# Attention reciprocals spread by TensorE transposes, scores copied to SBUF with their maximum, q and k loaded in 256 B pieces

## The chip, the cores and the metric

One core of a Trainium2 chip runs the whole program. The metric is device time in microseconds of one execution. The kernel before takes 2468.42 us, the median of 3 runs (2465.64 to 2470.5).

## The reference

Three parts follow each other. The attention has 4 batches of 8 heads, 576 positions, 64 features, and keeps only the scores near the row's maximum:

```
scores = scale * q @ k^T
thresh = max(scores) - tau
scores = where(scores >= thresh, scores, -1e9)
attn   = exp(scores - max) / (sum + 1e-9);   out = attn @ v
```

Its output, as a matrix of 2304 x 512, goes through a gated feed-forward layer (512 to 1536 to 512, with SiLU), and then through a layer of 8 experts (512 to 1024 to 512) that are mixed with weights normalised 8 times over rows and columns. All in fp32. The kernel does products of fp32 precision with two or three matmuls on a high and a low part of each operand.

## The kernel before, in words

The attention runs over 16 pairs of heads. Four heads (two pairs) are a group for loading: `load` brings q, k and v of a group from memory in DMAs issued on SP's queue (L247 for the first 512 positions of q and k, L260 to L273 for the 64 left and for v). 512 positions lie as 128 partitions of 4 positions each, which gives runs of 1 KB in memory.

For each pair, `add_prep` makes the operands of the score product. `relaid` (L333) copies q and k in SBUF so that the two heads lie side by side, on GpSimd (for the first pair on VectorE). TensorE transposes (L348), ScalarE evicts, GpSimd splits into a high and a low part (L397, L403), and DMAs on SP's queue (`spread_q` L431, `spread_k` L436) put the parts of the two heads where the score matmuls need them (`qs`, `kk`).

A pair has 9 tiles of 128 query rows by 576 keys. For each tile `qk` (L463) writes the scores to two PSUM banks, `smax` (L468, VectorE) takes the negated maximum, `thresh` (L471, GpSimd) the threshold, `sexp` (L475, ScalarE) the exponentials, and `mask` (L484, VectorE) multiplies the exponentials by the comparison and sums the row. Maximum, exponential and mask all read the scores in PSUM; there are two pairs of banks, so the scores of tile t+2 wait for the mask of tile t. The masked tile is transposed on TensorE (L552), evicted on ScalarE (`ev`, by the helper L194), and is then the moving operand of the product with v (L635).

The sums lie along partitions, one per query, while the output has queries along the free axis. So the reciprocals are turned into a row: after tiles 3 and 8 of a pair GpSimd adds the small constant (L496), VectorE takes reciprocals (L542), TensorE transposes two columns at a time (`pe_rows`, L594, L596) into two PSUM rows, one for each head, ScalarE copies them to SBUF (`rr`, `row_act` L520), and `row_sp` (L511) issues two DMAs on SP's queue, each of which broadcasts one row to 64 partitions (`rb`, 96 or 64 KB). GpSimd multiplies the output by `rb` on its way to the feed-forward layer's operand `xT` (L649).

The order of the work is written by a planner. `sch.add(kind, engine, cost, fn, deps, ring, frees)` enters a task; `run` simulates five in-order engines with these costs and emits on each the first task that can start, with ties within 0.1 us broken by a key from the table `PLAN` (a base for each kind, a step for its number within a pair, and 17.5 for each pair). All engines run what they get in order, and so does SP's one DMA queue. Three rings of PSUM banks (two pairs of banks for scores, two banks for transposes, two for the rest) are part of the plan. A conversion of the first layer's weights from 64 bit, in 72 VectorE operations (L832 to L841) with DMAs of its own, is threaded through the attention.

Behind attention, `gate_val`, `down`, `up` and `mix` run the two layers with a TensorE stream of matmuls at L862 to L864. Nothing in them is changed.

Of the kernel before, what the change touches and what calls it, by code (L numbers as in the profile page):

```python
# [19 lines left out]
P = 128  # L20
# [6 lines left out]
    both=(-33.85, 5.8), cv=(5.32, 3.279), cvl=(18.47, 1.707), cvs=(-39.34, 0.904), den=(-79.39, 9.964),  # L27
    eload=(107.14, 8.319), ev=(35.38, 1.15), exp=(14.18, 1.348), load=(-17.63, 2.381), mask=(-13.56, 3.546),
    max=(-8.59, 2.113), open=(25.4, -10.09), pk=(3.96, 1.461), pkm=(-11.67, -0.917), pkt=(-1.23, 1.982),
    pq=(0.82, -0.319), pqm=(-14.65, -4.23), pqt=(-4.27, -2.076), prod=(125.51, 1.066), ptail=(-21.32, 2.621),  # L30
    pv0=(11.01, -1.752), pv1=(44.19, 0.926), qk=(-13.11, 1.766), rec=(4.5, 8.216), rel=(-13.23, 0.628),
    row=(16.67, 9.817), rowa=(36.19, 15.901), rows=(-45.07, 15.448), scale0=(62.75, -0.384),
    scale1=(69.78, -1.611), spread=(-64.72, 0.436), tail=(8.48, 12.06), tev=(46.97, 5.187), thr=(-10.82, 4.603),
    tr=(8.8, 0.242), u0=(-82.36, 2.843), u1=(50.51, 0.091), warm=(-60.47, 4.548), wh=(-33.08, -0.513),
    wl=(18.21, -5.451), xh=(85.01, 0.401), xl=(71.1, -1.867),
# [96 lines left out]
def attention_moe_moe_kernel(  # L132
# [60 lines left out]
    def copy_act(o, i):  # L193
        nc.scalar.activation(out=o, in_=i, func=AF.Copy)  # L194
# [10 lines left out]
    def attention():  # L205
# [33 lines left out]
        def load(g):  # L239
# [5 lines left out]
            def main(i, n):  # L245
                for nm, src in (("q", q), ("k", k)):
                    nc.sync.dma_start(  # L247
                        d[nm][:, 2 * i:2 * (i + n)].rearrange("p h r d -> p h (r d)"),
                        src[b, h0 + 2 * i:h0 + 2 * (i + n), 0:MAIN, :].rearrange("h (p r) d -> p h (r d)", r=NR),
                    )  # L250

            def qk_first():
                for nm in "qk":
                    d[nm] = raw_p.tile([P, 4, NR, D], F32, tag=f"r{nm}", name=f"r{nm}{g}")
                main(0, 1 if g == 0 else 2)
# [9 lines left out]
            def rest():  # L265
                d["v"] = rv_p.tile([P, 4, NR, D], F32, tag="rv", name=f"rv{g}")
# [10 lines left out]
                if g == 0:  # L277
                    main(1, 1)
# [40 lines left out]
        hls, spread, qk_last, raw_used, rel_used, whole = {}, {}, {}, {}, {}, {}  # L319

        def add_prep(p):
            g, i = divmod(p, 2)
            d = raw[g]
            src, tl = loads[g][1 if g == 0 and i else 0], loads[g][2]
            h = hls[p] = {}
            old, free = spread.get(p - 1, ()), qk_last.get(p - 2)

            def relaid(nm):

                def fn():  # L330
                    x = h["rel", nm] = raw_p.tile([P, NR, 2, D], F32, tag=f"rel{nm}", name=f"rel{nm}{p}", bufs=1)
                    eng = nc.gpsimd if p else nc.vector
                    eng.tensor_copy(x, d[nm][:, 2 * i:2 * i + 2].rearrange("p h r d -> p r h d"))  # L333
                return sch.add("rel", *(("POOL", 0.62) if p else ("DVE", 0.7)), fn, [src, rel_used.get(nm)])

            def banks(parts):
                def fn():
# [6 lines left out]
                    for nm, off in parts:  # L344
                        h["ps", nm] = t
                        if nm in "qk":
                            for r in range(NR):
                                nc.tensor.transpose(t[:, r * P:(r + 1) * P], h["rel", nm][:, r].rearrange("p h d -> p (h d)"), ident)  # L348
# [69 lines left out]
            rq, rk = relaid("q"), relaid("k")  # L418
            t0 = sch.add("ptail", "PE", 0.25, banks([("qt", 0), ("kt", P)]), [tl], ring=ring_v)
            t1 = rel_used["q"] = sch.add("pqm", "PE", 0.44, banks([("q", 0)]), [rq], ring=ring_v)  # L420
            t2 = rel_used["k"] = sch.add("pkm", "PE", 0.44, banks([("k", 0)]), [rk], ring=ring_v)
# [44 lines left out]
        def smax(t):  # L466
            stat[t] = u_p.tile([P, 2], F32, tag="stat", name=f"st{t}", bufs=6)
            nc.vector.tensor_reduce(stat[t][:, 0:1], sc[t], axis=AX.XY, op=ALU.max, negate=True)  # L468

        def thresh(t):  # L470
            nc.gpsimd.tensor_tensor(stat[t][:, 1:2], ntau, stat[t][:, 0:1], op=ALU.subtract)  # L471

        def sexp(t):
            ee[t] = e_p.tile([P, 2, HS], F32, tag="ee", name=f"ee{t}")
            nc.scalar.activation(out=ee[t], in_=sc[t], func=AF.Exp, bias=stat[t][:, 0:1], scale=1.0)  # L475

        def mask(t):
# [3 lines left out]
            if s % 2 == 0:  # L481
# [3 lines left out]
                m, sc.pop(t), stat.pop(t)[:, 1:2], ee.pop(t), op0=ALU.is_ge, op1=ALU.mult,  # L485
# [21 lines left out]
        def row_sp(p, c, box, w):  # L507
            def fn():
                rb = rbt[p, c] = u_p.tile([P, w], F32, tag=f"rb{c}", name=f"rb{c}_{p}", bufs=1 + c)
                for h in range(2):  # L510
                    nc.sync.dma_start(  # L511
                        rb[h * 64:(h + 1) * 64, :],
# [713 lines left out]
```

## Time and profile before

| | before |
|---|---|
| median of 3 runs | 2468.42 us |
| the profiled execution's own time | 2469.57 us |
| span of its instructions | 2466.1 us |
| granted TensorE clock, mean | 0.985 |
| TensorE busy | 2383.1 us |
| VectorE busy | 1068.2 us |
| ScalarE busy | 647.9 us |
| GpSimd busy | 566.0 us |

The busy time of an engine is the union of its instructions. The DMA share is the time in which the core's 16 DMA engines had packets under way, as a mean. All DMAs of this kernel are issued by SP and share one queue, which each DMA engine works off in order. The first 410 us or so are attention.

### The profile page before, as it was taken

The numbers are of one execution on the slowest core, as the hardware profiler recorded it, in microseconds if no ns is written. First come the engines' busy times: TensorE is split into PE (matmuls) and PEld (weight loads), VectorE is DVE, ScalarE is ACT, GpSimd is POOL, SyncE is SP. The second block draws the span as 40 slices with busy tenths as digits, with TensorE's granted clock in tenths as the row PEclk, the third lists the DMA queues.
The fourth block names the chain that finished last, engine by engine and source line by source line (L and its number), as shares of the span: only waits on it lengthen the run. The fifth ranks groups of instructions, "written<-read, shape, count | busy, mean of one in ns | idle before, by whom it ended". The sixth has DMA issues, their size and how long they took to land.

```text
span 2466.1 us, 31099 instructions
## 1 busy us (share of the span) xinstructions
PE 2383.1 (97%) x12925; PEld 2151.7 (87%) x12925; DVE 1068.2 (43%) x1731; ACT 647.9 (26%) x1154; POOL 566.0 (23%) x599
## 2 busy tenths in 40 slices
PE   7887888999999999999999999999999999999999
PEld 6665666999999989999999999999999999999998
DVE  5765775565854214433333333333333333333333
ACT  4765664332223321111111111111111111111110
POOL 3553543545546500110110010010011011001000
PEclk8998999999999999999999999999999999999999
DMA  8888984111111000000000000000000000000002
GB/s 201 164 140 133 143 130 78 39 39 39 44 35 52 21 10 13 26 18 27 26 18 26 13 24 20 14 29 15 26 26 18 26 26 18 26 13 31 1 1 77
DMA packets 74172, 112.64 MB, mean 46 GB/s; under 512 B 12720, under 2 KB 50608, under 8 KB 74032
## 3 DMA queue, kind: packets, MB, share of 16 engines
q1 hardware_dynamic: 74032, 110.67, 20.4%
q8 instruction: 101, 1.65, 0.3%
q14 instruction: 39, 0.32, 0.0%
HBM read 68.96 MB, written 7.08 MB: 31 GB/s over the span
## 4 chain that ended last, share of the span: by engine, by line
PE 90%; DMA 5%; SPq 1%; DVE 1%; POOL 1%; issue 1%; ACT 1%; POOLq 0%; DVEq 0%; ACTq 0%
PE h L862 11%; PE h L864 11%; PE h L863 11%; PE y L863 11%; PE y L864 11%; PE y L862 11%; DMA rb<-rr 3%; PE pv L635 2%; PE s L463 2%; PE d L864 2%; PE d L863 2%; PE d L862 2%; PE v L862 2%; PE v L864 2%; PE v L863 2%; PE g L862 2%
## 5 line engine op out<-in xcount | busy, mean ns | idle before, releaser
L1125 ACT ACTIVATE hh<-h 128x384 fp32r<-128x384 f32 x384 | 188.8, 492 | 1194.3 <-PE h L864 1194.3
L1126 DVE SCALAR_TENSOR_TENSOR hl<-h,hh 128x384 fp32r<-128x384 f32 x384 | 213.9, 558 | 629.4 <-ACT hh L1125 629.2
L1160 DVE SCALAR_TENSOR_TENSOR acc<-y,gate_p,acc 128x512 f32<-128x512 f32 x378 | 283.8, 751 | 357.7 <-PE y L864 357.6
L484 DVE SCALAR_TENSOR_TENSOR em<-s,st,ee 128x576 f32<-128x576 f32 x144 | 115.9, 814 | 61.1 <-ACT ee L475 37.0
L463 PE MATMUL s<-kk,qs 128*128 128x288 f32 x512 | 104.2, 331 | 36.9 <-DMA kk<-khl 16.0
L468 DVE TENSOR_REDUCE st<-s 128x1 f32<-128x576 f32 x144 | 108.0, 755 | 54.0 <-PE s L463 52.2
L999 POOL TENSOR_TENSOR al<-av,ah 128x384 fp32r<-128x384 f32 x72 | 88.7, 1232 | 181.4 <-ACT ah L194 181.4
L463 PEld LDWEIGHTS s<-kk,qs 128*128 128x128 f32 x512 | 77.6, 202 | 59.5 <-issue 38.6
L552 PE MATMUL t<-ident,em 128*128 128x128 f32 x576 | 93.5, 295 | 27.9 <-ACT rr L194 26.9
L475 ACT ACTIVATE ee<-s,st 128x576 f32<-128x576 f32 x144 | 105.8, 741 | 33.3 <-DVE st L468 26.3
L997 DVE TENSOR_TENSOR av<-v,s 128x384 f32<-128x384 f32 x72 | 40.0, 556 | 159.7 <-PE v L864 143.1
L552 PEld LDWEIGHTS t<-ident,em 128*128 128x128 f32 x576 | 74.2, 151 | 38.8 <-ACT rr L194 29.7
L194 ACT ACTIVATE et<-t 128x512 f32<-128x512 f32 x144 | 83.3, 596 | 39.4 <-PE t L552 38.4
L194 ACT ACTIVATE ah<-av 128x384 fp32r<-128x384 f32 x72 | 37.8, 525 | 158.6 <-DVE av L997 158.6
L635 PE MATMUL pv<-et,rv 128*64 128x320 f32 (+1 forms) x512 | 78.4, 436 | 0.0
L471 POOL TENSOR_TENSOR st<-ntau,st 128x1 f32<-128x1 f32 x144 | 36.3, 256 | 91.2 <-DVE st L468 73.4
L635 PEld LDWEIGHTS pv<-et,rv 128*64 128x64 f32 x512 | 33.4, 143 | 25.5 <-issue 11.7
L1022 DVE TENSOR_TENSOR x<-d,x 128x384 f32<-128x384 f32 x72 | 39.4, 554 | 35.6 <-PE d L864 35.6
L995 ACT ACTIVATE s<-g 128x384 f32<-128x384 f32 x72 | 34.7, 482 | 75.3 <-PE g L864 75.2
L649 POOL TENSOR_TENSOR xT<-u,rb 64x64 f32<-64x64 f32 (+2 forms) x71 | 34.0, 497 | 23.6 <-DMA rb<-rr 22.4
L1156 DVE TENSOR_TENSOR acc<-y,acc 128x512 f32<-128x512 f32 x36 | 24.9, 692 | 32.2 <-PE y L864 32.2
L1028 POOL TENSOR_TENSOR x2l<-x,x2h 128x1536 fp32r<-128x1536 f32 x6 | 21.0, 3503 | 24.4 <-ACT x2h L194 24.4
(862 smaller groups left out, 6892.0 us busy)
## 6 DMA issues: line engine op xcount, KB each, us to landing
kk<-khl SPq DMA_DIRECT2D x64, 320.0 KB, 6.1
raw_a<-in_moe_w_dram SPq DMA_DIRECT2D x16, 768.0 KB, 4.5
raw_b<-in_moe_w_dram SPq DMA_DIRECT2D x16, 768.0 KB, 4.6
qs<-qhl SPq DMA_DIRECT2D x64, 128.0 KB, 4.1
raw_g<-in_moe_w_gate_dram SPq DMA_DIRECT2D x6, 768.0 KB, 4.8
raw_v<-in_moe_w_val_dram SPq DMA_DIRECT2D x6, 768.0 KB, 4.7
raw_o<-in_moe_w_out_dram SPq DMA_DIRECT2D x6, 768.0 KB, 4.3
rv<-in_v_dram SPq DMA_DIRECT2D x8, 512.0 KB, 6.2
```

Source lines behind the costliest of these rows:

```text
L194: nc.scalar.activation(out=o, in_=i, func=AF.Copy)
L463: nc.tensor.matmul(ps[:, n, 0:HS], lhs, rhs[:, ko + n * HS:ko + (n + 1) * HS], start=(x == 0), stop=(x == len(ops) - 1))
L468: nc.vector.tensor_reduce(stat[t][:, 0:1], sc[t], axis=AX.XY, op=ALU.max, negate=True)
L484: nc.vector.scalar_tensor_tensor(m, sc.pop(t), stat.pop(t)[:, 1:2], ee.pop(t), op0=ALU.is_ge, op1=ALU.mult, accum_out=sums[p][:, s:s + 1],)
L552: nc.tensor.transpose(ps[:, kb * P:(kb + 1) * P], em[p, s // 2][:, o:o + P], ident)
L635: nc.tensor.matmul(o, lhs, rhs, start=(kb == 0), stop=(kb == NR))
L862: nc.tensor.matmul(ps, a[0], b[0], start=start, stop=False)
L863: nc.tensor.matmul(ps, a[0], b[1], start=False, stop=False)
L864: nc.tensor.matmul(ps, a[1], b[0], start=False, stop=stop)
L1125: nc.scalar.activation(out=hh[:, f], in_=t[:, 0:BLK], func=AF.Relu)
L1126: nc.vector.scalar_tensor_tensor(hl[:, f], t[:, 0:BLK], 0.0, hh[:, f].bitcast(F32), op0=ALU.max, op1=ALU.subtract)
L1160: nc.vector.scalar_tensor_tensor(a, t, gate_p[:, i * NTB + n, e:e + 1], a, op0=ALU.mult, op1=ALU.add)
```

## The change

Four things are changed, and with them all numbers of `PLAN`.

1. GpSimd writes each reciprocal 64 times into a tile `wide` (`widen`, a new task `bc`). TensorE transposes this, so that the row comes out on all 128 partitions at once, and ScalarE copies it to `rb`. `row_sp` and its DMAs are gone; the scaling waits for ScalarE's copy.
2. `smax` writes the negated scores to SBUF (`ns`, two buffers) in the operation that finds the minimum of them. The exponentials and the mask read that copy. The bank is given back after this operation; it waits for the mask two tiles before, and the score product waits for the score product one tile before.
3. q and k are loaded into tiles in which the two heads already lie side by side, by one DMA for each head, with runs of 256 B in SBUF. `relaid` is gone; the transposes read the loaded tile.
4. Each group's second pair is loaded in the third step of `load`, ahead of v, in the first group and in all others.

```diff
-    both=(-33.85, 5.8), cv=(5.32, 3.279), ...
+    bc=(13.34, 8.915), both=(-23.93, 4.248), cv=(4.31, 1.393), ...
...
-                    nc.sync.dma_start(
-                        d[nm][:, 2 * i:2 * (i + n)].rearrange("p h r d -> p h (r d)"),
-                        src[b, h0 + 2 * i:h0 + 2 * (i + n), 0:MAIN, :].rearrange("h (p r) d -> p h (r d)", r=NR),
-                    )
+                    for h in range(2):
+                        nc.sync.dma_start(
+                            d[nm][:, i, :, h, :],
+                            src[b, h0 + 2 * i + h, 0:MAIN, :].rearrange("(p r) d -> p r d", r=NR),
+                        )
...
-            a = sch.add("load", "SP", 2 * 0.65, one, old, land=4.5)
+            a = sch.add("load", "SP", 4 * 0.65, one, old, land=4.5)
-            c = sch.add("load", "SP", (3 if g else 5) * 0.65, three, [a, *v_use.get(g - 2, ())], land=6.0)
+            c = sch.add("load", "SP", 7 * 0.65, three, [a, *old, *v_use.get(g - 2, ())], land=6.0)
...
-                    eng = nc.gpsimd if p else nc.vector
-                    eng.tensor_copy(x, d[nm][:, 2 * i:2 * i + 2].rearrange("p h r d -> p r h d"))
...
-            nc.vector.tensor_reduce(stat[t][:, 0:1], sc[t], axis=AX.XY, op=ALU.max, negate=True)
+            x = e_p.tile([P, 2, HS], F32, tag="ns", name=f"ns{t}", bufs=2)
+            nc.vector.tensor_scalar(x, sc[t], -1.0, None, op0=ALU.mult, op1=ALU.min, accum_out=stat[t][:, 0:1])
+            sc[t] = x
-            nc.gpsimd.tensor_tensor(stat[t][:, 1:2], ntau, stat[t][:, 0:1], op=ALU.subtract)
+            nc.gpsimd.tensor_tensor(stat[t][:, 1:2], stat[t][:, 0:1], ntau, op=ALU.subtract)
-            nc.scalar.activation(out=ee[t], in_=sc[t], func=AF.Exp, bias=stat[t][:, 0:1], scale=1.0)
+            nc.scalar.activation(out=ee[t], in_=sc[t], func=AF.Exp, bias=stat[t][:, 0:1], scale=-1.0)
-                m, sc.pop(t), stat.pop(t)[:, 1:2], ee.pop(t), op0=ALU.is_ge, op1=ALU.mult,
+                m, sc.pop(t), stat.pop(t)[:, 1:2], ee.pop(t), op0=ALU.is_le, op1=ALU.mult,
...
-                    nc.sync.dma_start(
-                        rb[h * 64:(h + 1) * 64, :],
-                        box["row"][h:h + 1, :].rearrange("a (o n) -> a o n", o=1).to_broadcast([1, 64, w]),
-                    )
+            x = wide[p, c] = u_p.tile([P, 2, 2, 64], F32, tag="wide", name=f"wide{p}_{c}", bufs=2)
+            r = recip[p, c][:, 0:4].rearrange("p (r h o) -> p r h o", h=2, o=1)
+            nc.gpsimd.tensor_copy(x, r.to_broadcast([P, 2, 2, 64]))
...
-                box["row"] = u_p.tile([2, w], F32, tag=f"rrow{c}", name=f"rr{c}_{p}", bufs=1)
-                copy_act(box["row"], box["rt"])
+                rbt[p, c] = u_p.tile([P, w], F32, tag=f"rb{c}", name=f"rb{c}_{p}", bufs=1 + c)
+                copy_act(rbt[p, c], box["rt"])
...
-            k_ = sch.add("qk", "PE", 0.54 if s < 8 else 0.8, lambda: qk(t), [*sq, masks.get(t - 2)], ring=ring_s)
+            k_ = sch.add("qk", "PE", 0.54 if s < 8 else 0.8, lambda: qk(t), [*sq, qks.get(t - 1)], ring=ring_s)
-            m_ = sch.add("max", "DVE", 0.77, lambda: smax(t), [k_])
+            m_ = sch.add("max", "DVE", 0.84, lambda: smax(t), [k_, masks.get(t - 2)], frees=(k_,))
...
-                    nc.tensor.transpose(rt[:, o + r * P:o + (r + 1) * P], rc[:, 2 * r:2 * r + 2], ident)
+                    nc.tensor.transpose(rt[:, o + r * P:o + (r + 1) * P], wide[p, c][:, r].rearrange("p h n -> p (h n)"), ident)
...
-                "rowa", "ACT", 0.38 if c == 0 else 0.47, row_act(p, c, box, w), [R_, h_, rows.get((p - 1, c))],
+                "rowa", "ACT", 0.38 if c == 0 else 0.47, row_act(p, c, box, w), [R_, h_, rb_free.get((p - 1 - c, c))],
```

## Rows read from the trace of the kernel before

**Rows 1.** The page: busy time of the engines, and DMA in 40 slices.

```profile
PE 2383.1 (97%) x12925; PEld 2151.7 (87%) x12925; DVE 1068.2 (43%) x1731; ACT 647.9 (26%) x1154; POOL 566.0 (23%) x599
...
DMA  8888984111111000000000000000000000000002
```

**Rows 2.** Stretches: us, busy us (instructions) by engine, granted clock, DMA share, GB/s.

```profile
20.00:395.00 375.00, 307.65 (x2082) 229.64 (x2084) 258.77 (x528) 238.98 (x461) 183.72 (x417) 0.91 0.85 141
60.00:80.00 20.00, 18.36 (x136) 13.74 (x136) 18.52 (x36) 15.37 (x29) 12.13 (x28) 1.00 0.76 142
160.00:180.00 20.00, 19.99 (x150) 15.09 (x149) 17.29 (x35) 16.24 (x34) 13.21 (x33) 1.00 0.85 154
300.00:340.00 40.00, 38.89 (x288) 28.95 (x289) 34.68 (x71) 31.71 (x63) 24.44 (x58) 1.00 0.90 143
```

**Rows 3.** The chain of waits from 20 to 410 us, shares by line.

```profile
by line: DMA rb<-rr 17.0%; PE pv L635 14.8%; PE s L463 14.6%; PE t L552 9.3%; DMA kk<-khl 9.1%; SPq L511 3.9%; issue 3.9%; DVE st L468 3.2%; DVE em L484 2.5%; DMA rv<-in_v_dram 2.0%; SPq L436 1.9%; DMA stage<-first_v 1.9%; PE tp L348 1.8%;
```

**Rows 4.** Waits, 0 to 420 us: who waited for whom, us, times, longest us.

```profile
ACT rr L194 <- DMA rb<-rr: 33.9, 11, 8.8
PEld t L552 <- ACT rr L194: 29.7, 7, 8.2
...
PE s L463 <- DVE em L484: 17.2, 19, 3.8
```

**Rows 5.** Timeline at 105 us: start, us, instruction, idle before it.

```profile
105.12 1.11 PE L552 MATMUL t<-ident,em 128*128 128x128 f32 x4 [4.34 <-ACT rr L194]
```

**Rows 6.** DMA: 0:420 (two issues), 0:410, 380:384, 10:12, 14:16 (last two lines).

```profile
rb<-rr SPq DMA_DIRECT2D x32, 96.0 KB, 8.3
rb<-rr SPq DMA_DIRECT2D x32, 64.0 KB, 7.9
...
q1 hardware_dynamic: 40762, 57.49, 82.8%
...
q1 hardware_dynamic: 88, 0.11, 88.6%
...
q1 hardware_dynamic: 743, 0.73, 107.3%
...
DMA packets 926, 0.58 MB, mean 288 GB/s; under 512 B 588, under 2 KB 835, under 8 KB 926
...
q1 hardware_dynamic: 926, 0.58, 115.4%
```

**Rows 7.** Groups of instructions, 0 to 420 us: busy us, mean ns, idle before.

```profile
L484 DVE SCALAR_TENSOR_TENSOR em<-s,st,ee 128x576 f32<-128x576 f32 x144 | 115.9, 814 | 61.1 <-ACT ee L475 37.0 <-POOL st L471 21.7 <-POOL khl L397 0.4
L468 DVE TENSOR_REDUCE st<-s 128x1 f32<-128x576 f32 x144 | 108.0, 755 | 54.0 <-PE s L463 52.2
...
L484 DVE DVE_READ_ACCUMULATOR em<-s,st,ee 128x1 f32 x144 | 11.9, 82 | 0.0
...
L333 POOL COPY relk<-rk 128x512 f32<-128x512 f32 x15 | 9.7, 644 | 1.2 <-PE tp L348 1.1
...
L582 PEld LDWEIGHTS tt<-ident,em 128*128 128x128 f32 x64 | 8.7, 151 | 1.0 <-ACT et L194 0.5 <-issue 0.4
...
L491 POOL COPY em<-em 128x64 f32<-128x64 f32 x16 | 3.8, 237 | 1.0
```

**Rows 8.** VectorE with two SBUF inputs (min/median/max ns), and the timeline at 302 us.

```profile
L840 DVE TENSOR_TENSOR cr<-cr x9: 687/936/1332, 19.2 to 367.1; 128x512 f32<-128x512 f32 x9
...
L841 DVE SCALAR_TENSOR_TENSOR ct<-cr,ct x9: 674/683/980, 26.2 to 369.6; 128x512 f32<-128x512 f32 x9
...
302.11 1.27 POOL L403 TENSOR_TENSOR khl<-raw_k,khl 128x512 fp32r<-128x512 f32 x1
302.60 1.33 DVE L840 TENSOR_TENSOR cr<-cr 128x512 f32<-128x512 f32 x1
```

More of the change, by code (lines that the diff above doesn't have):

```diff
@@ L26 @@
 PLAN = dict(
[L27 to L35, printed above, removed]
+    bc=(13.34, 8.915), both=(-23.93, 4.248), cv=(4.31, 1.393), cvl=(-33.33, 3.759), cvs=(77.26, -4.782),
+    den=(3.32, 8.309), eload=(88.68, 8.021), ev=(50.95, 0.72), exp=(10.43, 4.099), load=(-33.65, 0.373),
+    mask=(-8.56, 2.817), max=(-17.16, 2.219), open=(77.15, -15.53), pk=(-10.38, 0.874), pkm=(-6.48, -1.78),
+    pkt=(2.08, 0.668), pq=(9.51, 2.909), pqm=(-9.12, -0.109), pqt=(3.38, -9.918), prod=(82.35, 5.49),
+    ptail=(-15.04, 10.369), pv0=(15.24, -2.732), pv1=(43.41, 1.62), qk=(-9.54, 2.196), rec=(9.02, 7.443),
+    row=(23.67, 11.733), rowa=(-106.02, 17.482), scale0=(49.08, 6.001), scale1=(58.83, 0.3),
+    spread=(-3.96, 0.861), tail=(10.05, 8.173), tev=(52.42, 6.252), thr=(-6.58, 4.734), tr=(9.48, 0.17),
+    u0=(35.84, -4.942), u1=(40.2, 1.375), warm=(-43.13, 3.335), wh=(36.26, -1.299), wl=(83.87, -5.771),
+    xh=(62.3, -2.254), xl=(52.73, 1.861),
 )
@@ L312, in add_load @@
             old = qk_use.get(g - 2, ())
-            a = sch.add("load", "SP", 2 * 0.65, one, old, land=4.5)
+            a = sch.add("load", "SP", 4 * 0.65, one, old, land=4.5)
             b_ = sch.add("load", "SP", 3 * 0.65, two, old, land=4.5)
-            c = sch.add("load", "SP", (3 if g else 5) * 0.65, three, [a, *v_use.get(g - 2, ())], land=6.0)
+            c = sch.add("load", "SP", 7 * 0.65, three, [a, *old, *v_use.get(g - 2, ())], land=6.0)
             loads[g] = (a, c, b_)
-        hls, spread, qk_last, raw_used, rel_used, whole = {}, {}, {}, {}, {}, {}
+        hls, spread, qk_last, raw_used, whole = {}, {}, {}, {}, {}
         def add_prep(p):
@@ L347, in fn @@
                             for r in range(NR):
-                                nc.tensor.transpose(t[:, r * P:(r + 1) * P], h["rel", nm][:, r].rearrange("p h d -> p (h d)"), ident)
+                                nc.tensor.transpose(t[:, r * P:(r + 1) * P], d[nm][:, i, r].rearrange("p h d -> p (h d)"), ident)
                         elif nm == "qt":
@@ L442, in add_prep @@
             whole[p] = qt, km, kt
-            qk_use[g] = [t0, rq, rk]
-        masks, exps, em_free, et_free = {}, {}, {}, {}
+            qk_use[g] = [t0, t1, t2]
+        masks, exps, qks, em_free, et_free = {}, {}, {}, {}, {}
         sc, stat, ee, em, sums, et = {}, {}, {}, {}, {}, {}
-        recip, rows, rbt = {}, {}, {}
+        recip, wide, rows, rbt = {}, {}, {}, {}
         def qk(t):
@@ L536, in add_tile @@
             b = 5 * p + s // 2
-            masks[t] = mk = sch.add("mask", "DVE", 0.9, lambda: mask(t), [th, x_, masks.get(t - 1), *em_free.get(b - 4, ())], frees=(k_,))
+            masks[t] = mk = sch.add("mask", "DVE", 0.9, lambda: mask(t), [th, x_, masks.get(t - 1), *em_free.get(b - 4, ())])
             em_free.setdefault(b, [])
```

45 lines of the change are left out of this document (18 added, 27 removed).

## The prediction

> **What bounds the kernel now.** I read the 40 slices first. DMA engines stand at 8 to 9 tenths in the first six slices and fall to 1 or 0 from the eighth nearly to the end, while TensorE is busy 97% of the whole span [rows 1]. So there are two parts: the attention stage, some 410 us, and the two feed-forward layers, in which TensorE has no gap. The change touches only the first. What the second part costs after that is taken as it is: it begins when attention's last products are out, so a microsecond saved in attention is one saved at the end.
>
> Then the stretches. From 20 to 395 us (375 us, from the first scores to the last mask) TensorE is busy 307.65 us at a mean granted clock of 0.91 (a mix of its levels of 1.2 and 2.4 GHz), VectorE 258.77, ScalarE 238.98, GpSimd 183.72; the DMA engines show 85% [rows 2]. Nothing computes all the time. Yet there are clean pieces, 60 to 80, 160 to 180 and 300 to 340 us, where the clock is 1.00 (2.4 GHz) and 574 matmuls (136, 150, 288) pass in 80 us, 7.18 per us. At that rate the 2082 matmuls of the whole stretch take 2082 / 7.18 = 290 us. So 85 us are lost in the pieces between.
>
> The chain of waits says to what. Of the chain from 20 to 410 us, 17.0% is the DMA `rb<-rr` (the broadcast of the reciprocal row) and 3.9% its issue on SP's queue, L511 [rows 3]: 20.9% of 390 us is 82 us, which meets the 85. The list of waits shows how it reaches TensorE: ScalarE's copy of the next row (`rr`, one buffer) waits 33.9 us for the broadcast that still reads the old one; ScalarE runs in order, so the score evictions behind that copy stop, and TensorE's transposes wait for PSUM banks, 29.7 us at the weight load [rows 4]. One case, at 105.12 us, is 4.34 us of idle TensorE [rows 5].
>
> The broadcasts are slow for what they carry. From 380 to 384 us only they run: 88 packets and 0.11 MB occupy 88.6% of 16 engines for 4 us, 0.11 / (4 x 0.886) = 31 GB/s. All 64 carry 32 x 96 + 32 x 64 KB = 5.24 MB [rows 6], 169 us of all 16 engines, out of 82.8% of 410 = 339 us in the stage [rows 6]. Half of the DMA time goes to an eleventh of the stage's 57.49 MB.
>
> **The change, part by part.**
>
> *Rows by transposes.* The 64 broadcasts go, and with them the wait of `rr`, the 82 us of the chain and 169 us of DMA time. GpSimd widens the reciprocals instead, 32 copies of 256 elements a partition; the nearest rows are copies of 64 elements, 237 ns, and of 512, 644 ns [rows 7], so 8 to 21 us, say 13, on an engine that is busy half of the stretch. TensorE makes as many transposes as before with 128 weight columns instead of 2, and ScalarE copies 128 partitions instead of 2 with the same elements per partition; both taken as zero (up to 80 x 0.15 = 12 us on TensorE were a whole weight load exposed each time, which the overlap of loads and matmuls speaks against). New waits: TensorE's row transposes wait for the widening (mask, GpSimd, VectorE, GpSimd, TensorE), with all later products behind them; ScalarE's row copy waits for the scaling of the previous pair that still reads `rb`, with evictions and exponentials behind it. The scaling is GpSimd's last step of a pair and no DMA stands in it any more.
>
> *Scores copied by the maximum.* TensorE's bank is free after the maximum, not after the mask: 17.2 us of `s` waiting for `em` [rows 4] go or shrink. They are inside the 85 us. The next maximum must wait for the mask two tiles earlier (two `ns` buffers), which VectorE has run anyway. The price is VectorE's. The maximum now also reads out its accumulator, which takes 82 ns where the mask does it [rows 7]: 144 x 0.082 = 12 us; if the body also grows from the reduction's 755 to the mask's 814 ns, 8 more. I take 12. The mask now has two tensor inputs in SBUF. Before, one came from PSUM. Its body could fall to 755 ns (8 us less). But rows of such operations spread: L840 takes 687 ns at least, 936 in the median and 1332 at most, L841 674, 683 and 980 [rows 8]; the 1.33 us one, at 302.60, began while GpSimd's 1.27 us subtraction from 302.11 ran [rows 8]. Excess of the median: 0.009 to 0.249 us; times 144, 1 to 36 us, and 93 us at L840's worst. I take the middle, 0.13 us, 19 us.
>
> The Trainium skill has a rule on this (SBUF — State Buffer, section "Who interferes with whom"): a VectorE instruction with two SBUF inputs contends with a GpSimd instruction that reads SBUF, and the later one waits until the first is through. The trace agrees in the pair at 302 us. By that rule GpSimd's small thresholds are also held up by masks, which the sum doesn't charge; what the rule would do at its worst is the slower rival below.
>
> *256 B loads.* The re-laying copies on GpSimd go, 30 of about 0.64 us [rows 7], 19 us for the 13 added; GpSimd is not late, so no gain. Each later group of two pairs loads q and k as 4096 packets of 256 B instead of 1024 of 1 KB. From 10 to 12 us, 1 KB packets: 107.3% x 2 x 16 / 743 = 46 ns each. From 14 to 16 us, 588 of 926 packets are small; 115.4% x 32 = 36.9 us less 338 x 46 ns leaves at most 36 ns for a small one [rows 6]; at the byte rate of the large ones it would be 11.5. Taken: 23 ns. A group goes from 1024 x 46 / 16 = 2.9 to 4096 x 23 / 16 = 5.9 us of all engines, 21 us over seven groups (nothing to 44). In one queue this stands in front of the spreads of q and k, which the matmuls wait for; with 169 us of broadcasts gone I charge a quarter as exposed, 5 us. SP issues 8 DMAs where it issued 2, but loses 8 broadcasts for the same group. The first group's extra loading and its two copies saved at the start are set against each other (3 us either way).
>
> The skill's page DMA: Bandwidth & Descriptors, "Specifications", says that transfers under 512 B don't reach the line rate; the packets from 14 to 16 us don't contradict it, and by it the upper end of 36 ns would be the likelier, and the sum 2427 instead of 2421.6 (a quarter of 44 us exposed, not of 21).
>
> **The sum.** TensorE could do the stretch in 290 us. VectorE now has 258.8 + 12 + 19 = 290 us of work, and is busy at best 18.52 of 20 us, 70.5 of 80 (88%) in the clean pieces [rows 2]. At 90% it needs 322 us: it is late next, not TensorE. So 375 becomes 322, a gain of 53, less 5 for the loads: 48. The profiled execution took 2469.57 us, so 2421.6; it is 1.2 above the median of the runs shown, 2468.42. Forecast 2421 us.
>
> **Rivals.** *TensorE stays the bound* (mask free of contention, loads hidden): the stretch falls to 290 us, 85 gained, 2385 us. For it: in the clean pieces TensorE is the fuller engine. Against: VectorE would have to be busy at 93% or more.
>
> *Loads clog the queue.* At 36 ns a packet a group costs 9.2 us, 6.3 more than before; seven of them wholly in front of spreads take 44 of the 53 us back: 2461 us. For it: spreads already wait in that one queue behind loads at 85% occupancy. Against: half of that occupancy leaves.
>
> *Slower: masks behind GpSimd.* Place: VectorE's mask, 144 times. At 0.55 us excess each (between L840's median and its worst) VectorE has 258.8 + 12 + 79 = 350 us of work; at 90% 389 us, 14 more than 375: 2483 us. It decides from (0.9 x 375 - 271) / 144 = 0.46 us per mask on. For it: GpSimd is busy 49% of the stretch. Against: L841, the nearest form, has a median only 9 ns over its least.
>
> *It doesn't do what it says*: TensorE waits for the widening as it waited for the broadcast. 32 row steps would have to lose 2.5 us each to eat 82 us; the new hop is one copy of under 0.65 us. Held in the second rival's chance.
>
> **Chances.** Forecast (2405 to 2440) 0.50, TensorE bound 0.20, loads 0.20, slower 0.10. What a measurement can tell from no change is 0.2%, 5 us. A little of the second and of the third rival's edge falls within: faster 0.87, same 0.04, slower 0.09. The range runs from 2388 to 2455: it takes in most of TensorE's case and the half-exposed loads, and leaves out the slower one.
>
> **What would show it.** Attention's last mask at about 345 us instead of 395; no chain share of `rb`; DMA share of the stage near 50 to 60%; the waits of `rr` and of `t` on ScalarE gone; VectorE at 85 to 93% and in the chain; the mask's mean at 0.8 to 1.05 us. The clock should be nearer to 1.00, since TensorE idles less. Wrong: if the mask's mean passes 1.27 us, if the spreads `kk` take more than 8 us to land in the middle of the stage, or if TensorE's row transposes carry long waits on the widening.

## The result, and the profile after

The changed kernel takes 2410.97 us (median of four runs, 2410.57 to 2413.97) where the kernel before took 2467.61 (2465.64 to 2470.5) beside it: a ratio of 0.9772, 95% interval [0.9755, 0.9789], 57 us less. The forecast was 2421 us, range 2388 to 2455. The profiled execution took 2410.57 us with a span of 2408.5 and a mean granted clock of 0.995 (before: 2469.57, 2466.1 and 0.985).

The page of the changed kernel, busy time and the DMA engines in 40 slices, against [rows 1]:

```profile
PE 2365.5 (98%) x12925; PEld 2141.9 (89%) x12925; DVE 1097.1 (46%) x1873; ACT 652.8 (27%) x1154; POOL 628.9 (26%) x601
...
DMA  8666632010110100000000000000000000000002
```

After the first slice the DMA engines stand at 6, not 8 to 9, and attention is over about a slice (60 us) earlier. TensorE has the same 12925 matmuls. VectorE has 29 us more work and GpSimd 63 us more, although GpSimd lost the 19 us of re-laying copies and gained only the 18 us of widening.

The last mask shows the end of attention. The row gives the mask's least, median and largest duration in ns, then first and last start in us:

```profile
L478 DVE SCALAR_TENSOR_TENSOR em<-ns,st,ee x144: 802/819/1870, 24.3 to 338.3; 128x576 f32<-128x576 f32 x144
```

The same of the kernel before:

```profile
L484 DVE SCALAR_TENSOR_TENSOR em<-s,st,ee x144: 798/817/820, 23.3 to 394.1; 128x576 f32<-128x576 f32 x144
```

The last mask starts at 338.3 us instead of 394.1. That is 55.8 of the 57.6 us by which the span is shorter, so the feed-forward layers behind it take as long as they did.

Stretches of the changed kernel (us; busy us and instructions of TensorE, its weight loads, VectorE, ScalarE, GpSimd; granted clock, DMA share, GB/s), against [rows 2]:

```profile
20.00:340.00 320.00, 291.96 (x2102) 220.96 (x2102) 284.83 (x668) 243.84 (x462) 249.46 (x424) 0.97 0.66 154
60.00:300.00 240.00, 224.14 (x1650) 170.41 (x1648) 217.89 (x508) 188.84 (x362) 194.46 (x334) 0.99 0.66 153
20.00:60.00 40.00, 31.96 (x198) 25.74 (x200) 29.92 (x75) 24.26 (x45) 25.14 (x43) 0.83 0.91 210
```

What took 375 us takes 320. VectorE is busy 284.83 / 320 = 89% and GpSimd 78% (before 69% and 49% of the 375). In the middle, 1650 / 240 = 6.88 matmuls pass per us. The first 40 us are still slow: 198 matmuls at a granted clock of 0.83, DMA engines at 91%. The middle piece of the kernel before, for the comparisons below, is 1385 / 240 = 5.77 per us:

```profile
60.00:300.00 240.00, 201.31 (x1385) 148.13 (x1384) 164.53 (x335) 156.64 (x304) 122.11 (x280) 0.92 0.87 145
```

The chain of waits from 20 to 352 us, shares by line, against [rows 3]:

```profile
by line: PE s L454 10.1%; PE pv L626 9.5%; issue 7.9%; POOL xT L640 6.6%; PE t L544 6.6%; DMA kk<-khl 5.2%; POOL st L465 4.7%; POOL khl L395 4.4%; POOL qhl L395 4.3%; POOL qhl L389 3.4%; ACT ee L469 3.0%; SPq L427 3.0%; DVE em L478 2.5%; PO
```

No broadcast is left in it. In its place stand small shares of everything, and GpSimd (xT, st, khl, qhl) has 23.4% in this one line, VectorE's mask 2.5%.

Waits of the changed kernel from 0 to 360 us (us, times, longest us), against [rows 4]:

```profile
POOL st L465 <- DVE ns L461: 52.0, 49, 21.6
...
ACT rb L194 <- PE tr L588: 16.5, 9, 8.0
PEld s L454 <- DVE ns L461: 14.1, 20, 1.3
...
PEld tr L586 <- POOL wide L505: 10.2, 10, 1.9
...
PE tr L586 <- POOL wide L505: 7.7, 7, 1.7
```

The waits of `rr` for the broadcast and of `t` for `rr` are gone. The new hop over GpSimd's widening shows 10.2 us of waits at the weight load and 7.7 at the matmul, never over 1.9 us at once.

Groups from 0 to 360 us (busy us, mean ns, idle before), against [rows 7]:

```profile
L478 DVE SCALAR_TENSOR_TENSOR em<-ns,st,ee 128x576 f32<-128x576 f32 x144 | 138.3, 960 | 12.6 <-POOL st L465 8.2 <-ACT ee L469 3.6 <-POOL qthl L389 0.3
L461 DVE TENSOR_SCALAR_CACHE_REDUCE ns<-s 128x576 f32<-128x576 f32 x144 | 108.3, 752 | 17.2 <-PE s L454 11.2
L465 POOL TENSOR_TENSOR st<-st,ntau 128x1 f32<-128x1 f32 x144 | 67.9, 471 | 53.4 <-DVE ns L461 52.0
L505 POOL COPY wide<-rec 128x256 f32<-128x256 f32 x32 | 18.2, 569 | 5.5 <-DVE rec L533 4.2 <-PE s L454 0.4 <-PE t L544 0.4
L389 POOL TENSOR_SCALAR qhl<-raw_q 128x512 fp32r<-128x512 f32 x15 | 14.2, 948 | 0.0
L461 DVE DVE_READ_ACCUMULATOR ns<-s 128x1 f32 x144 | 11.6, 81 | 0.0
```

The mask has grown from 814 to 960 ns, its least and median have not (802 and 819): a part of the 144 is held up, one for 1870 ns. The maximum that also copies 576 scores a partition has the body of the plain one, 752 against 755 ns, plus an accumulator read of 81 ns. GpSimd's threshold, one element a partition, went from 256 to 471 ns, and the high part of q (L397 before) from 647 to 948.

DMA of the changed kernel, 0 to 350 us (packets, MB, share of 16 engines), against [rows 6]:

```profile
q1 hardware_dynamic: 61088, 52.97, 64.7%
```

64.7% of 350 us is 226 us of 16 engines, where it was 339.

### The profile page after: what moved, and what is told of

It is laid out like the page before. It is cut to its first block, busy times and chain, and to the rows that moved or that the text cites. A ratio compares the mean times of both kernels' runs of the same rounds, so it can differ in the third digit from the quotient of the medians.

```text
span 2408.5 us, 31221 instructions
## 1 busy us (share of the span) xinstructions
PE 2365.5 (98%) x12925; PEld 2141.9 (89%) x12925; DVE 1097.1 (46%) x1873; ACT 652.8 (27%) x1154; POOL 628.9 (26%) x601
## 4 chain that ended last, share of the span: by engine, by line
PE 90%; POOL 5%; issue 1%; DMA 1%; ACT 1%; DVE 1%; SPq 1%; POOLq 0%; DVEq 0%; ACTq 0%
PE h L853 11%; PE h L855 11%; PE h L854 11%; PE y L854 11%; PE y L855 11%; PE y L853 11%; PE d L854 2%; PE d L855 2%; PE d L853 2%; PE v L853 2%; PE v L854 2%; PE v L855 2%; PE g L853 2%; PE g L854 2%; PE g L855 2%; PE s L454 1%
## 5 line engine op out<-in xcount | busy, mean ns | idle before, releaser
L478 DVE SCALAR_TENSOR_TENSOR em<-ns,st,ee 128x576 f32<-128x576 f32 x144 | 138.3, 960 | 12.6 <-POOL st L465 8.2
L469 ACT ACTIVATE ee<-ns,st 128x576 f32<-128x576 f32 x144 | 111.6, 775 | 32.1 <-DVE ns L461 31.2
L461 DVE TENSOR_SCALAR_CACHE_REDUCE ns<-s 128x576 f32<-128x576 f32 x144 | 108.3, 752 | 17.2 <-PE s L454 11.2
L544 PE MATMUL t<-ident,em 128*128 128x128 f32 x576 | 85.6, 280 | 3.1 <-ACT et L194 2.2
L465 POOL TENSOR_TENSOR st<-st,ntau 128x1 f32<-128x1 f32 x144 | 67.9, 471 | 53.4 <-DVE ns L461 52.0
L544 PEld LDWEIGHTS t<-ident,em 128*128 128x128 f32 x576 | 67.9, 143 | 11.6 <-ACT et L194 5.3
L640 POOL TENSOR_TENSOR xT<-u,rb 64x64 f32<-64x64 f32 (+2 forms) x71 | 46.0, 661 | 4.4 <-ACT u L194 3.2
```

The source lines that it names most:

```text
L461: nc.vector.tensor_scalar(x, sc[t], -1.0, None, op0=ALU.mult, op1=ALU.min, accum_out=stat[t][:, 0:1])
L478: nc.vector.scalar_tensor_tensor(m, sc.pop(t), stat.pop(t)[:, 1:2], ee.pop(t), op0=ALU.is_le, op1=ALU.mult, accum_out=sums[p][:, s:s + 1],)
L544: nc.tensor.transpose(ps[:, kb * P:(kb + 1) * P], em[p, s // 2][:, o:o + P], ident)
```

## The experiments

Theory: the broadcasts are the loss, and taking them away is the whole gain; copied scores and small packets cost what the sum charges. Rivals: the copied scores free banks and carry part of the gain; VectorE's contention sets the new end; or the time is made by the planner, which writes a new order for every edit. The last one had no term in the prediction, and the runs brought it up.

Twelve kernels ran, each with runs of the kernel before beside it on the same chip (before: 2466.6 to 2469.8 us).

| kernel | median us | ratio to before [95%] |
|---|---|---|
| the changed kernel | 2410.97 | 0.9772 [0.9755, 0.9789] |
| a1: changed, rows by DMA | 2498.88 | 1.0121 [1.0106, 1.0136] |
| a2: changed, scores in PSUM | 2435.81 | 0.9865 [0.9849, 0.9882] |
| a4: changed, mask reads PSUM | 2430.85 | 0.9847 [0.9832, 0.9861] |
| b1: before, rows by transposes, old table | 2473.38 | 1.0023 [1.0014, 1.0032] |
| d3: before, rows by transposes, new table | 2429.54 | 0.9849 [0.9835, 0.9862] |
| d1: changed, old table | 2457.46 | 0.9963 [0.9949, 0.9977] |
| p1: changed, 1 KB runs | 2407.28 | 0.9763 [0.9750, 0.9776] |
| c1: changed, threshold on ScalarE | 2468.31 | 1.0004 [0.9995, 1.0013] |
| r1: before, rows by transposes, same order | 2407.89 | 0.9756 [0.9742, 0.9771] |
| r3: changed, rows by DMA, same order | 2495.78 | 1.0113 [1.0098, 1.0128] |
| r2: changed, threshold on ScalarE, same order | 2405.02 | 0.9744 [0.9728, 0.9761] |
| r4: whole change, order of before | 2436.07 | 0.9864 [0.9844, 0.9884] |

### a1, a2, a4: parts of the change undone

a1 gives the changed kernel its broadcasts back:

```diff
-            nc.gpsimd.tensor_copy(x, r.to_broadcast([P, 2, 2, 64]))
+                    nc.sync.dma_start(
+                        rb[h * 64:(h + 1) * 64, :],
+                        box["row"][h:h + 1, :].rearrange("a (o n) -> a o n", o=1).to_broadcast([1, 64, w]),
+                    )
```

> The changed kernel with the reciprocal rows brought to the partitions by DMA broadcasts again; scores copied to SBUF and 256 B loads stay. Theory (the broadcasts are the loss: 64 of them hold the DMA engines about 169 us and ScalarE behind them): the stretch goes back to 375 us or more, 2465 to 2490 us, DMA share of the stage 0.85 or more, ScalarE's row copy waits for the broadcast again. Rival (the gain is the PSUM bank given back at the maximum): most of the gain stays, 2425 to 2440 us.

Measured 2498.88 us: 88 more than the changed kernel, 30 more than before, and 9 above the range that was expected. The planner wrote a new order for it, so these figures price the broadcasts and an order together; r3 below holds the order. One expected sign didn't come: ScalarE's row copy never waits for a broadcast here. GpSimd's scaling does, 27.1 us in all.

a2 leaves the scores in PSUM until the mask:

```diff
-            nc.vector.tensor_scalar(x, sc[t], -1.0, None, op0=ALU.mult, op1=ALU.min, accum_out=stat[t][:, 0:1])
-            sc[t] = x
+            nc.vector.tensor_reduce(stat[t][:, 0:1], sc[t], axis=AX.XY, op=ALU.max, negate=True)
```

> The changed kernel with maximum, exponentials and mask reading the scores in PSUM again, the bank held until the mask; rows by transposes and 256 B loads stay. Theory (once the broadcasts are gone VectorE and GpSimd are the bound, and the copy costs VectorE 12 us of accumulator reads and 21 us of mask, and GpSimd much more): mask back at 814 ns, threshold on GpSimd back near 256 ns, GpSimd busy under 190 us, time equal or better, 2385 to 2412 us. Rival (the bank given back early carries part of the gain): TensorE waits for the mask, 2425 to 2445 us.

a4 keeps the copy for the exponential, but the mask reads the scores in PSUM, so that it has one SBUF input; the bank is held until the mask:

```diff
-                m, sc.pop(t), stat.pop(t)[:, 1:2], ee.pop(t), op0=ALU.is_le, op1=ALU.mult,
+                m, scp.pop(t), stat.pop(t)[:, 1:2], ee.pop(t), op0=ALU.is_ge, op1=ALU.mult,
```

> The changed kernel in which only the mask reads the scores in PSUM again (exponentials still read the copy), so that the mask has one SBUF input and the bank is held until the mask. Theory (the mask's second SBUF input is what slows it and GpSimd): mask 960 to about 815 ns, GpSimd's threshold 471 to about 260 ns, GpSimd busy in the stretch 249 to under 200 us; the time follows whichever is larger, the 21 us of VectorE won or the bank held longer: 2390 to 2425 us. Rival (GpSimd is slower for another reason, its own added work): threshold stays above 400 ns.

2435.81 and 2430.85 us, 25 and 20 more than the changed kernel; the first is in the rival's range, the second above both ranges. In these two, VectorE's relief is worth less than what came with it. But both were planned anew, so the times alone don't say whether held banks or the order did it. What a4 does settle is the contention. Its groups from 0 to 360 us:

```profile
L478 DVE SCALAR_TENSOR_TENSOR em<-s,st,ee 128x576 f32<-128x576 f32 x144 | 116.1, 814 | 31.7 <-ACT ee L469 14.6 <-POOL st L465 13.5 <-POOL khl L389 2.1
...
L465 POOL TENSOR_TENSOR st<-ntau,st 128x1 f32<-128x1 f32 x144 | 31.4, 221 | 99.3 <-DVE ns L461 90.7 <-DVE rec L532 7.8
...
L389 POOL TENSOR_SCALAR qhl<-raw_q 128x512 fp32r<-128x512 f32 x15 | 9.7, 650 | 0.5
```

With one SBUF input the mask is back at 814 ns, and GpSimd's threshold falls from 471 to 221 ns, its high part of q from 948 to 650. a4 also holds the bank longer and has another order, so here are the thresholds one by one (least, median and largest ns), of the changed kernel and then of a4:

```profile
L465 POOL TENSOR_TENSOR st<-st,ntau x144: 179/627/752, 23.4 to 336.7; 128x1 f32<-128x1 f32 x144
```

```profile
L465 POOL TENSOR_TENSOR st<-ntau,st x144: 183/192/742, 24.2 to 354.1; 128x1 f32<-128x1 f32 x144
```

Sorted by when they start, the traces leave no room for the order as the cause. In the changed kernel 69 thresholds start while a mask runs and take 698 ns in the median; the 75 others take 189. The medians inside a mask are 698 to 701 ns in all six kernels with two SBUF inputs and the threshold on GpSimd (the changed one, a1, d1, p1, r3, r4), and 189 to 192 in all six whose mask has one (before, a2, a4, b1, d3, r1). Nor does any mask of the latter six take over 820 ns, while every kernel with two inputs has masks over 1800. So the mask's second SBUF input is what slows both engines, and the order sets how often they meet. The Trainium skill (SBUF — State Buffer, section "Who interferes with whom") says that a VectorE instruction with at most one SBUF input, outside its two-port modes, doesn't contend with GpSimd, and that one with two SBUF inputs contends with a GpSimd instruction that reads SBUF. These rows agree with it.

### b1, d3, d1: the rows alone, and the planner's table

b1 does the rows alone on the kernel before, with its table of keys and a guessed key for the new task; d3 is b1 with the table of the changed kernel; d1 is the changed kernel with the old table.

```diff
 PLAN = dict(
+    bc=(5.0, 8.5),
...
-    r_ = sch.add("rowa", "ACT", ...)
-    rows[p, c] = sch.add("rows", "SP", 1.3, row_sp(p, c, box, w), [r_, rb_free.get((p - 1 - c, c))])
+    bc = sch.add("bc", "POOL", 0.35, lambda: widen(p, c), [rec])
+    rows[p, c] = sch.add("rowa", "ACT", ..., row_act(p, c, box, w), [R_, h_, rb_free.get((p - 1 - c, c))])
```

> The kernel before with one part of the change alone: reciprocals widened on GpSimd and transposed by TensorE, no broadcasts. Theory: all or more than the whole gain, 2385 to 2415 us, since VectorE keeps its 259 us of work. Rival (only the parts together gain): 2435 to 2460 us.

> The kernel before with the rows by transposes alone, but with the new table of keys (the old key for the re-laying). Scores in PSUM until the mask, 1 KB loads with re-laying. Theory (rows plus an order that suits them is the larger half): 2425 to 2445 us, near the 2436 of rows and 256 B loads without the copied scores. Rival (rows without the other parts gain nothing in any order): 2460 to 2480 us.

> The changed kernel with the old table of keys (and a key of 5.0, 8.5 for the new widening): same work, another order. Theory (the order written by the planner is a bound of its own once the broadcasts are gone; rows alone with the old table gained nothing, TensorE taking the products with v of two pairs in one run of 40 while VectorE waited): most of the gain is lost, 2445 to 2475 us, with VectorE's masks waiting for TensorE. Rival (the order matters little, the parts carry the gain together): 2405 to 2425 us.

b1 was a miss for the theory and above the rival's range too: 2473.38 us, no gain at all, though no broadcast is left and the DMA share of 20 to 340 us fell to 0.54. d3, the same work in another order, takes 2429.54. d1, the whole change in an order by the old table, takes 2457.46, 46 more than the same work by the new one. Waits of b1, 0 to 380 us:

```profile
POOL rec L496 <- DVE em L484: 50.1, 16, 4.7
...
DVE em L484 <- PE tt L579: 41.5, 12, 4.3
```

and one such wait in its timeline (start, us):

```profile
99.92 1.14 PE L549 MATMUL t<-ident,em 128*128 128x128 f32 x8 [0.53 <-ACT et L194]
...
101.27 0.44 PE L579 MATMUL tt<-ident,em 128*128 128x128 f32 x2 [0.20 <-ACT et L194]
...
101.70 0.82 DVE L484 SCALAR_TENSOR_TENSOR em<-s,st,ee 128x576 f32<-128x576 f32 x1 [3.16 <-PE tt L579]
```

In this order TensorE's tail transposes (`tt`) come late, here behind 16 transposes of masked scores and 4 of the next pair's operands. They free the buffer that the next mask writes, so the masks wait 41.5 us for them. The same wait takes 33.8 us in d1 and 59.6 in c1 below, the other two orders that lose most or all of the gain; before, the changed kernel and d3 don't have it. That it makes the whole loss isn't shown. (The expectation of d1 blames a run of 40 products with v. b1 and d1 have such runs, but c1 has none over 20.) So a planned comparison prices two things at once, and an edit has to be priced with the order held.

### r1 and r3: the rows with the order held

For these, the order in which a kernel issues its operations was recorded and replayed. r1 is the kernel before with the rows by transposes, everything else in before's order, the widening right behind its reciprocal, and two buffers instead of one for the shorter `rb`. r3 is the changed kernel in its own order with the broadcasts back behind the row copy.

```diff
     def run(self):
-        ... (the planner)
+        todo = {(t.kind, t.pair, t.n): t for t in self.tasks}
+        for key in recorded():
+            todo.pop(key).fn()
```

> The kernel before with the rows by transposes alone, every other task in exactly the order in which the kernel before has it (the planner's order is written down and replayed; the widening stands right behind the reciprocal, ScalarE's row copy keeps its place, two buffers of the row for both halves). Theory (the broadcasts are the 82 us of the chain; the 2473 of rows alone came from the new order that the planner made of it): 2385 to 2420 us. Rival (without the other parts nothing is gained, in any order): 2440 to 2475 us.

> The changed kernel with the rows brought by DMA broadcasts, every other task in exactly the order of the changed kernel (the two broadcasts are issued right behind ScalarE's row copy). Theory (the broadcasts cost their wait and 169 us of DMA time in this order too): 2465 to 2500 us. Rival (the 2499 of the kernel with its own order was that order): 2425 to 2450 us.

r1 takes 2407.89 us: the rows alone give 60 us, as much as the whole change. (The second `rb` buffer wasn't priced by itself; the changed kernel and r3 do without it.) Stretches and chain (20 to 340 us) of r1:

```profile
20.00:340.00 320.00, 296.96 (x2121) 223.07 (x2122) 266.25 (x536) 240.68 (x464) 196.93 (x451) 0.98 0.61 151
60.00:300.00 240.00, 232.53 (x1696) 172.15 (x1694) 205.54 (x412) 190.42 (x370) 157.43 (x364) 1.00 0.62 154
20.00:60.00 40.00, 28.27 (x170) 23.78 (x170) 30.09 (x62) 21.34 (x40) 17.77 (x41) 0.80 0.80 194
```

```profile
by line: PE s L497 18.3%; PE pv L665 13.5%; PE t L583 9.5%; issue 7.3%; DVE st L502 5.0%; POOL khl L437 4.6%; DMA kk<-khl 4.3%; DVE em L518 4.1%; POOL qhl L437 3.5%; POOL st L505 3.3%; POOL khl L431 2.7%; PE tp L382 2.5%; ACT ee L509 2.3%; 
...
35.62 9.28 DMA kk<-khl
```

Its last mask (0 to 420 us) and its queue (0 to 350 us):

```profile
L518 DVE SCALAR_TENSOR_TENSOR em<-s,st,ee x144: 798/817/819, 25.3 to 334.4; 128x576 f32<-128x576 f32 x144
...
q1 hardware_dynamic: 35646, 52.27, 59.9%
```

(The recorded order stands in the file, so lines are 34 further down.) In the middle TensorE is busy 97%, at a granted clock of 1.00 (2.4 GHz), and does 1696 / 240 = 7.07 matmuls per us, near the 7.18 of the clean pieces; it leads the chain. The first 40 us stay slow; one spread `kk` stands in that part of the chain with 9.28 us.

r3 takes 2495.78 us, 85 more than the changed kernel. Its chain from 20 to 340 us, and the stretch:

```profile
by line: DMA kk<-khl 16.7%; PE s L488 13.9%; PE t L581 10.4%; DMA rb<-rr 10.2%; PE pv L664 9.9%; issue 8.4%; DVE em L512 3.4%; SPq L461 3.0%; PE tp L374 2.7%; SPq L539 2.7%; ACT ee L503 2.4%; POOL xT L678 2.3%; DVE ns L495 2.2%; ACT et L228
```

```profile
60.00:300.00 240.00, 192.64 (x1351) 147.16 (x1352) 172.49 (x420) 154.34 (x298) 143.68 (x253) 0.91 0.88 141
```

The broadcasts take the DMA engines from 66% to 88% and the middle from 6.88 to 5.63 matmuls per us. Much of their harm is indirect here: the spreads `kk`, which share their queue, have 16.7% of the chain (5.2% in the changed kernel), the broadcasts themselves 10.2%. The wait for a broadcast is another engine's (0 to 400 us):

```profile
POOL xT L678 <- DMA rb<-rr: 35.3, 11, 8.1
```

ScalarE, which waited 33.9 us for the broadcasts in the kernel before [rows 4], doesn't wait for one here. So the single `rr` buffer isn't needed for the loss. What a second one would have given the kernel before wasn't run.

### c1 and r2: the threshold taken from GpSimd

GpSimd's threshold stands between each maximum and its mask. Both kernels compute it on ScalarE, c1 planned anew (with another key for the threshold), r2 in the changed kernel's recorded order with the threshold right ahead of the exponential.

```diff
-    thr=(-6.58, 4.734)
+    thr=(10.0, 4.09)
...
-            nc.gpsimd.tensor_tensor(stat[t][:, 1:2], stat[t][:, 0:1], ntau, op=ALU.subtract)
+            nc.scalar.activation(out=stat[t][:, 1:2], in_=stat[t][:, 0:1], func=AF.Identity, bias=ptau, scale=1.0)
```

> The changed kernel with the mask's threshold computed on ScalarE instead of GpSimd (144 instructions of one element; key 10.0, 4.09). It takes 68 us of work off GpSimd, where it waits behind masks, and adds some 30 us to ScalarE's 244. Theory (GpSimd at 78% with VectorE's two-input masks is in the chain, 27% of it): 2385 to 2408 us. Rival (ScalarE's in-order queue becomes the bound, the exponentials stand behind thresholds): 2412 to 2435 us.

> The changed kernel with the mask's threshold on ScalarE, right in front of the tile's exponentials, every other task in exactly the order of the changed kernel. The 2468 of the same edit with the planner's own order had TensorE's tail transposes late and masks waiting for them, as all kernels with a poor order. Theory (GpSimd's 249 us in the stretch and its blocked thresholds are in the chain): GpSimd falls to about 180 us, 2390 to 2406 us. Rival (each exponential starts 0.3 us later and ScalarE fills up, which costs what GpSimd gives): 2408 to 2425 us.

c1 loses all of the change's gain (2468.31 us, above both of its ranges), with the mask waiting for tail transposes again (0 to 400 us):

```profile
DVE em L480 <- PE tt L576: 59.6, 20, 5.8
```

r2 takes 2405.02: the same edit, 63 us apart by its order alone. Against the changed kernel r2 is 6 us less, with intervals that overlap; it has the lowest median of all runs. Stretch and groups of r2:

```profile
60.00:300.00 240.00, 230.11 (x1712) 173.56 (x1711) 226.57 (x528) 214.20 (x489) 162.52 (x233) 1.00 0.65 156
```

```profile
L514 DVE SCALAR_TENSOR_TENSOR em<-ns,st,ee 128x576 f32<-128x576 f32 x144 | 140.9, 978 | 3.7 <-ACT ee L505 2.9
...
L501 ACT ACTIVATE st<-st,ptau 128x1 f32<-128x1 f32 x144 | 42.3, 294 | 22.7 <-DVE ns L497 21.1
```

The mask is no faster (978 ns), so VectorE has as much to do, but it is busy 226.57 / 240 = 94%, where it was 91%, and TensorE does 7.13 matmuls per us instead of 6.88. So VectorE alone wasn't the limit of the changed kernel. That it waited for a GpSimd that was 81% busy in this piece fits both traces, but 6 us are too few to call it shown.

### p1: packets of 1 KB at the same bytes and number of DMAs

```diff
-                            d[nm][:, i, :, h, :],
-                            src[b, h0 + 2 * i + h, 0:MAIN, :].rearrange("(p r) d -> p r d", r=NR),
+                            d[nm][:, i].rearrange("p r h d -> p (r h d)")[:, h * NR * D:(h + 1) * NR * D],
+                            src[b, h0 + 2 * i + h, 0:MAIN, :].rearrange("(p r) d -> p (r d)", r=NR),
```

> The changed kernel with the same eight loads a group and the same bytes of q and k, but each head's 1 KB left in one run in SBUF, so that the two heads are not interleaved (the attention is computed on wrongly ordered features; what is left out is the interleaving). It prices the 256 B packets. Theory (23 ns a packet, a quarter of it exposed): DMA share of the stage falls by some 6 points, time 2401 to 2411 us, 0 to 0.3% less. Rival (36 ns packets clog the queue in front of the spreads): 2380 to 2398 us.

p1 leaves out the interleaving of the two heads. It takes 2407.28 us, 3.7 less than the changed kernel (2 by the ratios), with overlapping intervals. The queue of p1, 0 to 350 us:

```profile
q1 hardware_dynamic: 36545, 53.02, 61.5%
```

24543 packets fewer and 64.7 - 61.5 = 3.2% of 350 us, 11 us of 16 engines, less. With 8192 packets of 1 KB at 46 ns [rows 6] in place of 32768 small ones, a small one takes (11.2 x 16000 + 8192 x 46) / 32768 = 17 ns, an estimate that hangs on the 46. Four of them cost 68 ns where one large one costs 46. On the end of the kernel this is worth so little that the two can't be told apart.

### r4: the whole change in before's order

r4 is the changed kernel, replayed in before's order, with one buffer for the widened rows and two for `rb`, and the second pair's loads beside the first's.

```diff
-            x = wide[p, c] = u_p.tile([P, 2, 2, 64], F32, tag="wide", name=f"wide{p}_{c}", bufs=2)
+            x = wide[p, c] = u_p.tile([P, 2, 2, 64], F32, tag="wide", name=f"wide{p}_{c}", bufs=1)
...
-                rbt[p, c] = u_p.tile([P, w], F32, tag=f"rb{c}", name=f"rb{c}_{p}", bufs=1 + c)
+                rbt[p, c] = u_p.tile([P, w], F32, tag=f"rb{c}", name=f"rb{c}_{p}", bufs=2)
```

> The whole change (rows by transposes, copied scores, 256 B loads), but every operation in the order in which the kernel before issues them (the widening right behind its reciprocal, the re-laying left out, one buffer for the widened rows so that two hold the broadcast rows). Beside the rows alone in that same order, at 2408 us, it prices the copied scores and the loads together with no re-planning in it. Theory A (what the copy and the contention add to VectorE, 33 us, is hidden while TensorE bounds the stretch; the price is what the rows-alone run and the changed kernel differ by, 0 to 5 us): 2405 to 2416 us. Theory B (the 33 us show, and only the new order hides them): 2430 to 2445. Theory C (copied scores free banks and let TensorE run ahead, which the order written for held banks can use as well): under 2404.

2436.07 us, 28 more than r1 (27 by the ratios): theory B. Its middle stretch:

```profile
60.00:300.00 240.00, 220.46 (x1577) 159.06 (x1574) 207.06 (x492) 180.18 (x346) 163.07 (x319) 1.00 0.63 149
```

6.57 matmuls per us, with TensorE at 92%, VectorE at 86% and GpSimd at 68%: no engine is full. The copied scores and the small loads are not free; their 28 us show in an order that was written for other durations. In the changed kernel's own order the same work takes 25 us less. The single `wide` buffer isn't the main reason: GpSimd's widening waits 5.3 us in all for TensorE to release it. Which of the engines' turns loses the rest wasn't taken apart.

Not tried: the copied scores alone on the kernel before, the 1 KB loads with re-laying in the changed kernel, and the rows alone in the changed kernel's order, which would say what the other parts cost in that order.

## Why the prediction was right, step by step

**The bound before: right.** Broadcasts were the loss. Put back into the changed kernel with its order kept, they cost 85 us (r3); taken from the kernel before with its order kept, they give 60 (r1). The path by way of ScalarE's `rr` is the one of the kernel before. In r3 the harm comes by the queue instead, through `kk` and GpSimd's scaling, so that r3's 85 and the forecast's 85 are alike by chance.

**TensorE's 290 us: too low.** The step "at that rate the 2082 matmuls of the whole stretch take 290 us" took every slow piece for the broadcasts' doing. r1 has neither broadcasts nor the copied scores, runs at 7.07 per us in the middle, and its last mask still ends at 335.2 us, 315 us after 20. Of these 25 us, the first 40 us of the stretch make 16: 170 matmuls where 287 would pass at 7.18, 117 / 7.18 = 16 us. The middle from 60 to 300 us makes 4 (1696 / 7.18 = 236), and the rest is its end. The first 40 us are slow in the kernel before as well (180 matmuls) and after (198), with the DMA engines at 80 to 91% and a granted clock of 0.79 to 0.83. I read this as the fill of the pipeline, one `kk` spread of which takes 9.28 us in r1; no run takes it apart. So the rows were worth 60 and not 85, and the chain's 82 us, which met the 85, were no measure of the gain either.

**DMA time of the broadcasts: too high.** 169 us came from 88 packets of one short piece. r1's queue has 59.9% of 350 = 210 us at 52.27 MB, which is before's 57.49 less the broadcasts' 5.24 to within 0.02; 339 - 210 = 129 us went with them. This is why the share ended at 64.7% (r1 59.9%) and not between 50 and 60.

**Widening: small, as held.** 18.2 us of GpSimd instead of 13 (569 ns each; 480 in r1, where no mask contends). The row transposes wait for it, but for under 2 us at a time, inside what the forecast called no long wait. ScalarE's row copy waits 16.5 us for the transposes, 8.0 of them once, behind the last mask. TensorE's and ScalarE's own share, taken as zero, can't be seen: 64 row weight loads at about 141 ns, inside the matmuls.

**VectorE's terms: right.** The accumulator read cost 144 x 81 ns = 11.6 us (12 forecast). The maximum's body didn't grow. The mask's excess is 960 - 814 = 146 ns, 21 us (0.13 us, 19). At 89% busy the stretch ended at 339.1 us; 290 us at 90% had put it at 342.

**What these terms cost: not as the sum had it.** The forecast charged 32 us for VectorE's fill above TensorE's 290, and 5 for the loads: 37. Between r1 and the changed kernel there are 3 us, but these two have different orders. In r1's order there are 28 (r4). So the price exists there, near the forecast's 37, and a new order took 25 us back; whether it hides the price or gains elsewhere isn't shown. The two mis-sized terms offset each other: -85 + 37 = -48 was forecast, -60 + 3 = -57 measured. The forecast held an order fixed that the planner writes anew, and had no term for it. That it came as near as 10 us is in good part luck.

**"VectorE is late next": half right.** It is the fullest engine but one, at the share that was forecast. But it doesn't lead the chain, and r2 raised it to 94% in the middle without touching its work. What the traces suggest as the bound is the loop from the maximum over GpSimd's threshold to the mask; r2's 6 us are too few to show it. The sum didn't charge GpSimd's side of the contention: 144 thresholds at 471 instead of 256 ns are 31 us, and its other operations are longer as well, from 4% (the low part of q, 1278 to 1323 ns) to 47% (the high part, 647 to 948).

**The loads: right in sign, smaller.** 11 us of DMA time where 21 were taken (17 ns a packet, bounds 11.5 to 36, 23 taken), and at the end 2 to 4 us within the noise where 5 were charged. The Trainium skill (DMA: Bandwidth & Descriptors, section "Specifications") has transfers under 512 B below the line rate, by which the forecast called 36 ns the likelier end. The trace agrees with the direction, since 256 B at 17 ns move fewer bytes per ns than 1 KB at 46, but not with that end.

**The rivals.** *TensorE stays the bound*: r1 and nearly r2 are that case, but at 2405 to 2408 us, not 2385, since the fill stays. *Loads clog the queue*: no; `kk` lands in 4.7 us in the median, before in 6.1. *Masks behind GpSimd*: the mechanism is there, at 146 ns a mask in the mean where it needed 460. *It doesn't do what it says*: no.

## What to carry to other kernels

In this kernel the transfers that stood in a queue in front of others cost more than their own wait. Look for the transfers with few bytes and much engine time, and see whether an engine that has gaps can do their work. Before a part is priced by undoing it, hold the order of all other operations: the same edit gave 2473, 2430 and 2408 us in three orders, which is more than the change itself. And the rate of a stretch's clean pieces held for its middle here, but not for its start.

## What the runs showed of the hardware

- A mask with two SBUF inputs slows GpSimd more than itself. In the mean, the changed kernel against a4: 146 ns on 814 for the mask (median unchanged, longest 1870), 250 ns on 221 for a threshold of one element a partition, 300 ns on 650 for the high part of q, 128x512. A threshold that starts during such a mask takes 698 ns in the median, one that starts outside 189.
- A `tensor_scalar` that writes 128x576 from PSUM to SBUF and accumulates a minimum takes 752 ns, the plain reduction 755; beside it stands an accumulator read of 81 ns.
- By estimate from p1 and [rows 6], packets of 256 B from memory took some 17 ns of a DMA engine and those of 1 KB 46 ns.
- The 64 broadcasts of a row to 64 partitions, 5.24 MB, went with 129 us of all 16 DMA engines (before against r1).
